# Fourier part: sequence first, and three of its seven products by seven smaller ones

## The chip, the core and the metric

The kernel runs on one core of a Trainium2 chip. The core has a matrix engine (TensorE, PE in the profile), three engines for element-wise work (VectorE or DVE, ScalarE or ACT, GpSimd or POOL), and a queue engine (SyncE or SP), which starts all of this kernel's transfers between HBM and the on-chip memory. The engines follow their own instruction lists and meet at semaphores. The metric is the device time of one execution in microseconds, the median of several runs.

## The reference, cut to what matters

Two independent computations are laid side by side in the output. All arrays are float32; S is 2048 and D is 1024.

```python
def _A_ref(x, wqkv, wo):                       # attention, 32 heads of 32
    qkv = (x @ wqkv).reshape(B, S, 3, H, Dh).transpose(2, 0, 3, 1, 4)
    q, k, v = qkv[0], qkv[1], qkv[2]
    p = _softmax(jnp.einsum("bhqd,bhkd->bhqk", q, k) * Dh ** -0.5)
    o = jnp.einsum("bhqk,bhkd->bhqd", p, v)
    return o.transpose(0, 2, 1, 3).reshape(B, S, D) @ wo

def _B_ref(x, dft_seq_re, dft_seq_im, dft_hid_re, dft_hid_im):   # Fourier mixing
    a = jnp.einsum("bsd,ed->bse", x, dft_hid_re)
    b = jnp.einsum("bsd,ed->bse", x, dft_hid_im)
    return jnp.einsum("ts,bse->bte", dft_seq_re, a) - jnp.einsum("ts,bse->bte", dft_seq_im, b)

return jnp.concatenate([_A_ref(...), _B_ref(...)], axis=-1)      # [1, 2048, 2048]
```

The Fourier part is the real part of (Cr + i Ci) X (Wr + i Wi), where X is 2048 x 1024, Cr and Ci are 2048 x 2048 and Wr and Wi are 1024 x 1024. It can be summed over the hidden dimension first, or over the sequence first.

## The kernel before

**Number form.** Each float32 operand of a large product is held as a high and a low half in a shortened float format (fp32r). One term of a product, a 128 x 128 block by a 128 x 512 block, is three matmuls: high by high, low by high, high by low. The halves are made by `halves`: a cast (line 528 on DVE, line 527 on ACT) and a subtraction (line 531 on POOL or DVE). `fetch` loads a block (line 491) and, where an operand is a sum of blocks, loads the others (line 500) and adds them (line 507 on POOL or DVE).

**Fast products.** Each large product is cut into 2 x 2 quarters and made with seven quarter products instead of eight, after Strassen and Winograd. This takes sums of operand quarters ahead of the products and sums of results behind them (`gather`).

**Stages.** Four pieces of matrix work are recorded in one long list, the fills: `qkv` (2016 matmuls), `dense1` (X by Wr and Wi, 448 terms, 1344 matmuls), `dense2` (Cr and Ci by the two results, 896 terms, 2688 matmuls) and `project` (the output projection of attention, 672 matmuls): 6720 in all. In the two Fourier stages a group of 12 or 24 matmuls sums one 128 x 512 result in a bank of PSUM, which DVE then drains. Operands, partial results and the result of `dense1` go through HBM buffers by transfers of 256 KB.

**Attention.** For every head two kinds of score matmuls are made (line 1322 for the row maxima, line 1447 for the exponentials), 4096 in all, and the products with V (line 1479), in 72 visits. DVE finds maxima, ACT takes exponentials, and both free the score banks.

**The order of the work.** A planner (`Plan`) is run when the program is recorded. It has a cost for each instruction, gives each engine's next instruction when its inputs will be there by these costs, and writes the engines' instruction lists. On PE it chooses at each step between the next fill and the next attention matmul; the fills are paced by `nf / (FILL - RES) <= done / ATT`, so that they last nearly as long as attention. On the chip the lists are fixed and every wait is a semaphore.

**The end.** `project` needs all heads. Its operand tiles use memory that attention held, so none of its loads may start before the last head's result is stored (`behind`, line 1519 stores it). Between the last visit to V and the first matmul of `project` PE has only what is left of `dense2`. `project` makes its seven products in the order 1, 7, 2, 6, 5, 3, 4, each with 8 groups of 12 matmuls. Product 1 uses eight tiles of the heads' outputs (`o_d`) and four of the weight (`wo`) as they are; for product 7 each of its eight and four tiles is a difference of two loaded blocks.

## Time and profile before

| | |
|---|---|
| median of 3 timed runs | 2941.32 us (2941.31 to 2941.8) |
| the profiled execution: span from its first to its last instruction | 2940.6 us |
| granted TensorE clock over the span | 1.000 |
| PE busy, share of the span | 2931.5 us, 100% |
| DVE, ACT, POOL busy | 77%, 77%, 33% |
| transfers | 587.96 MB, 61.8% of the 16 DMA engines' span |

The profiled execution's own time is known by its span; the lowest timed run is 0.7 us longer than that, which is what lies around the span. In the views, "PE" rows are matmuls and "PEld" rows the loading of their fixed operand. A matmul's listed duration (about 390 ns) is longer than its share of the engine, since matmuls overlap; the distance from one to the next is what counts. In a table by stretches, each engine has its busy time and, in brackets, its number of instructions; the last three columns are the granted clock, the busy share of the DMA engines and GB/s. Most groups carry the line of a helper: 421 is every product's matmul, whatever its stage.

### The profile page before, as it was taken

The page shows a single profiled execution, that of the slowest core. Times are in us where ns is not written, and L with a number is a line of the kernel's source. Part 1 is how long each engine was busy: PE and PEld are TensorE (multiplying, and loading weights), DVE is VectorE, ACT ScalarE, POOL GpSimd, SP SyncE. Part 2 cuts the span into 40 slices and gives each one's busy share as a digit, 9 for nine tenths or more (in the row PEclk, how much of TensorE's full clock was granted, in tenths as well). Part 3 has the DMA queues.
Part 4 walks back from the last instruction along what each step waited for, and adds up shares of the span by engine and source line. Part 5 has one row for each costly group of instructions (what it writes and reads, how often), then busy time and mean ns, then how long its engine had stood idle before and what let it go on. Part 6 is the DMA issues. An engine that isn't in the chain of part 4 may idle for free.

```text
span 2940.6 us, 45778 instructions
## 1 busy us (share of the span) xinstructions
PE 2931.5 (100%) x14922; PEld 2151.9 (73%) x14922; DVE 2275.1 (77%) x3103; ACT 2271.7 (77%) x4322; POOL 956.6 (33%) x746
## 2 busy tenths in 40 slices
...
GB/s 348 356 249 183 200 183 276 227 213 225 218 103 229 217 176 164 212 226 166 158 101 147 239 231 205 189 180 169 129 113 132 216 270 200 194 182 191 264 194 126
DMA packets 393880, 587.96 MB, mean 200 GB/s; under 512 B 112782, under 2 KB 114574, under 8 KB 393518
## 3 DMA queue, kind: packets, MB, share of 16 engines
q1 hardware_dynamic: 393644, 585.05, 61.8%
...
## 4 chain that ended last, share of the span: by engine, by line
PE 98%; DVE 1%; DMA 1%; ACT 0%; SPq 0%; issue 0%; DVEq 0%; ACTq 0%
PE pd L421 44%; PE psT L1447 16%; PE psS L1322 16%; PE pd L1479 15%; PE psT L421 6%; DVE negm L1328 0%; DMA er<-in_xa 0%; DVE l L531 0%; DMA qs<-qk_d 0%; PE psT L443 0%; ACT psS L1331 0%; DVE h L528 0%; PE pd L443 0%; ACT slot L527 0%; DVE slot L531 0%
## 5 line engine op out<-in xcount | busy, mean ns | idle before, releaser
L1328 DVE TENSOR_REDUCE negm<-psS 128x1 f32<-128x1024 f32 x1024 | 1242.8, 1221 | 226.4 <-PE psS L1322 215.2
L1331 ACT ACTIVATE psS<-psS,negm 128x1024 f32<-128x1024 f32 x1024 | 1223.9, 1195 | 71.8 <-DVE negm L1328 70.0
L421 PE MATMUL pd<-slot,h 128*128 128x512 f32 x3360 | 1144.0, 390 | 0.0
L1456 ACT ACTIVATE pt<-psT 128x512 f32<-128x512 f32 x1296 | 782.6, 697 | 260.1 <-PE psT L1447 237.2
L1447 PE MATMUL psT<-qs,ks 128*128 128x512 f32 x2048 | 794.3, 394 | 1.3 <-DMA qs<-qk_d 1.3
L421 PEld LDWEIGHTS pd<-slot,h 128*128 128x128 f32 x3360 | 630.7, 188 | 132.0
L421 PE MATMUL pd<-slot,l 128*128 128x512 f32 x1680 | 654.6, 390 | 0.0
L507 POOL TENSOR_TENSOR raw<-raw,g 128x512 f32<-128x512 f32 x295 | 382.6, 1304 | 483.8 <-DVE l L531 63.8
L1447 PEld LDWEIGHTS psT<-qs,ks 128*128 128x128 f32 x2048 | 381.8, 188 | 137.3 <-issue 45.3
L1322 PE MATMUL psS<-ks,qs 128*128 128x512 f32 x1552 | 473.4, 390 | 1.2 <-ACT psS L1331 1.2
L531 POOL TENSOR_TENSOR l<-raw,h 128x512 fp32r<-128x512 f32 x157 | 202.5, 1290 | 554.6 <-PE psT L1447 236.6
L531 POOL TENSOR_TENSOR slot<-raw,slot 128x512 fp32r<-128x512 f32 x156 | 201.0, 1293 | 518.0 <-DVE slot L528 146.3
L421 PEld LDWEIGHTS pd<-slot,l 128*128 128x128 f32 x1680 | 315.3, 188 | 67.0 <-issue 0.8
L1479 PE MATMUL pd<-pt,vt 128*32 128x512 f32 x2592 | 345.8, 594 | 0.0
L1322 PEld LDWEIGHTS psS<-ks,qs 128*128 128x128 f32 x1552 | 290.8, 188 | 64.0 <-ACT psS L1331 3.8
L1331 ACT ACTIVATION_READ_ACCUMULATOR psS<-psS,negm 128x1 f32 x1024 | 321.6, 314 | 0.0
L1456 ACT ACTIVATE ptm<-psT 128x512 f32<-128x512 f32 x392 | 242.6, 715 | 49.7 <-PE psT L1447 46.7
L1456 ACT ACTIVATE ptl<-psT 128x512 f32<-128x512 f32 x360 | 223.5, 708 | 31.0 <-PE psT L1447 30.2
L1479 PEld LDWEIGHTS pd<-pt,vt 128*32 128x32 f32 x2592 | 89.4, 110 | 180.3 <-issue 168.2
L421 PE MATMUL pd<-slot,slot 128*128 128x512 f32 x768 | 193.0, 391 | 0.0
L421 PEld LDWEIGHTS pd<-slot,slot 128*128 128x128 f32 x768 | 144.1, 188 | 31.2
L528 DVE CAST h<-raw 128x512 fp32r<-128x512 f32 x321 | 149.1, 467 | 14.5 <-PE pd L421 12.3
...
## 6 DMA issues: line engine op xcount, KB each, us to landing
...
g<-in_ct SPq DMA_DIRECT2D x128, 256.0 KB
...
qs<-qk_d SPq DMA_DIRECT2D x128, 192.0 KB
ks<-qk_d SPq DMA_DIRECT2D x128, 192.0 KB
...
```

What stands on the lines that cost most here:

```text
L421: nc.tensor.matmul(box["ps"], a[1]((a[0].hi, a[0].lo)[u]()), b[1]((b[0].hi, b[0].lo)[v]()), start=k == 0, stop=k == n - 1)
L507: return (nc.gpsimd if e == "POOL" else nc.vector).tensor_tensor(out=dest(), in0=dest() if a is None else a.get(), in1=other["q"] if "q" i ...
L528: return nc.vector.tensor_copy(hi(), raw())
L531: return (nc.gpsimd if e == "POOL" else nc.vector).tensor_tensor(out=lo(), in0=raw(), in1=f(hi()), op=ALU.subtract)
L1322: nc.tensor.matmul(p[:, i * NB : i * NB + NB], (QX[0] if own else QS[h % 2])[:, qt * P : qt * P + P], KS[h % 2][:, c * 1024 + i * NB : c * ...
L1328: nc.vector.tensor_reduce(out=ST["negm"][:, c, qt : qt + 1], in_=box["p"], axis=AX.X, op=ALU.max, negate=True)
L1331: nc.scalar.activation(box["p"], box["p"], AF.Exp, bias=ST["negm"][:, c, qt : qt + 1], accum_out=ST["sums"][:, c, qt : qt + 1])
L1447: nc.tensor.matmul(box["p"], KS[h % 2][:, t * P : t * P + P], QS[h % 2][:, j * NB : j * NB + NB], start=True, stop=True)
L1456: nc.scalar.activation(box["t"], box["p"], AF.Exp)
L1479: nc.tensor.matmul(po["p"][j * DH : j * DH + DH, :], VT[h][:, k, :], box["t"], start=(k == t0), stop=(k == t), tile_position=(0, j * DH),)
```

## The change

**What it does.** `dense1` now sums over the sequence: it makes U = X^T C^T for both Cr and Ci, a product of 1024 x 2048 by 2048 x 4096, whose result is stored in `ut_d` (the half of Ci with its sign turned). `dense2` then multiplies U^T by Wr and Wi, one product of 2048 x 2048 by 2048 x 1024, and its result goes to the output with no intermediate `y_d`. Together the two stages would again have 896 + 448 terms. Three of the seven products of `dense1` (`SPLIT = (1, 2, 3)`) are not made directly, in 4 x 4 groups of 8 terms (`simple`), but by seven products of their own quarters (`split`), in 7 x 2 x 2 groups of 4 terms: 112 terms in place of 128. The other four products keep their fixed operand, all eight tiles of it, on chip for the four column blocks (`held`). The running sums of the outer products go through HBM (`xx_d`, `yy_d`), the sums of the inner ones stay on chip. The pacing counts a fill of a split product 1.5 times (`HEAVY`), and casts may go to ACT there (`spare`).

```diff
-    ab_d = [[[dram.tile([P, NB], F32, name=f"ab_d{m}_{e}_{k}") for k in range(NS)] for e in range(2)] for m in range(2)]
-    y_d = [[dram.tile([P, NB], F32, name=f"y_d{i}_{e}") for e in range(2)] for i in range(NS)]
+
+    ut_d = [[[dram.tile([4, P, 4, P], F32, name=f"ut_d{e}_{n}_{r}") for r in range(2)] for n in range(4)] for e in range(2)]
...
-    FILL = 3 * (7 * 24 * 4 + 7 * 16 * 4 + 7 * 8 * 16 + 2 * 8 * 4)
+    SPLIT = (1, 2, 3)
+    HEAVY = 1.5
+    FILL = 3 * (7 * 24 * 4 + 7 * 16 * 8 - 16 * len(SPLIT) + 7 * 8 * 8 + 2 * 8 * 4)
...
-                fills.append((o, k == 0, n - k))
+                fills.append((o, k == 0, n - k, heavy[0]))
...
+    def merge(dst, acc, ps, kind, neg):
+
+        if not neg:
+            nc.vector.tensor_tensor(out=dst, in0=acc, in1=ps, op=kind)
+        elif kind == ALU.add:
+            nc.vector.scalar_tensor_tensor(out=dst, in0=ps, scalar=-1.0, in1=acc, op0=ALU.mult, op1=ALU.subtract)
+        else:
+            nc.vector.tensor_tensor(out=dst, in0=ps, in1=acc, op=ALU.subtract)
+
+    def put_out(to, t):
+
+        nc.sync.dma_start(to, t.rearrange("p (b j) -> p b j", b=4) if len(to.shape) == 3 else t)
...
+    def inner(j, x, y, outer, last_of):
...
+        def finish(ps, last):
+            def acc(A, B):
...
+            if j == 1:
+                return acc(x, None)
+            if j == 5:
+                return acc(y, x)
+            if j == 6:
+                acc(x, x)
+                return acc(y, y)
+            also = [acc(x, x)] if j == 7 else []
+            a = x if j in (2, 4) else y
+            box = {}
+            old, users = ER.take()
+
+            def emit():
+                box["y"] = pre.tile([P, NB], F32, name="e", tag="e", bufs=NE)
+                merge(box["y"], a.at(), ps(), ALU.subtract if j == 4 else ALU.add, outer[0] == 3)
+
+            e = done = evac_op(emit, last, ER, [users, a.users], [*old, a.last, *also])
+            if outer[0] != 1:
+                done = op("POOL", SUB, lambda e: (nc.gpsimd if e == "POOL" else nc.vector).tensor_tensor(
+                    out=box["y"], in0=box["y"], in1=got["c"], op=ALU.subtract if outer[0] == 3 else ALU.add),
+                    [e, c], [users, cusers], rank, other=("DVE", ADD, 20 + rank), two=True)
+            stored = op("SP", ISSUE, lambda: put_out(outer[2], box["y"]), [done], [users], rank, 256)
+            if outer[0] == 1:
...
+    def split_a(p, q, s1, s2):
+        return {
+            1: [(1, *q(0, 0))], 2: [(1, *q(0, 1))], 4: [(1, *q(1, 1))],
+            5: [(1, *q(1, 0)), (1, *q(1, 1))],
+            6: [(1, *s1), (-1, *q(0, 0))],
+            7: [(1, *q(0, 0)), (-1, *q(1, 0))],
+            3: [(1, *q(0, 1)), (-1, *s2)],
+        }[p]
+
+    def split_b(p, q, t1, t2):
...
+    OUTER = (1, 5, 2, 6, 7, 4, 3)
+    WITHIN = (1, 2, 5, 6, 7, 3, 4)
+    DONE_IN = {2: (0, 0), 7: (1, 1), 3: (0, 1), 4: (1, 0)}
...
+    def outer(p, X, Y, to, wrote, neg):
...
+        x = stored(X.first if p == 2 else X.kept) if p in (2, 4, 5, 6, 7) else None
+        y = stored(Y.kept) if p in (3, 6, 7) else None
...
+            if p == 1:
+                e = result(None, None, False, X.to[1], X)
+                X.first = X.kept
+                return e
+            if p == 5:
+                return result(x, ALU.add, False, Y.to[5], Y)
+            if p == 6:
+                result(x, ALU.add, False, X.to[6], X)
+                return result(y, ALU.add, False, Y.to[6], Y)
+            if p == 7:
+                result(y, ALU.add, neg, to, None)
+                return result(x, ALU.add, False, X.to[7], X)
+            return result(y if p == 3 else x, ALU.subtract if p == 4 else ALU.add, neg, to, None)
+
+        return finish
...
+    def dense1():
...
+        def to(h, m, n):
+            return ut_d[h[1]][n][h[0]][:, :, m, :].rearrange("b p j -> p b j"), ut_st[h[1]][n][h[0]]
...
+        def simple(p):
+            def a(m, k):
+                q = lambda r, kk: xq(4 * r + m, 8 * kk + 4 * k)
+                return split_a(p, q, (s1_d[m][k], s1[m][k]), (s2_d[m][k], s2[m][k]))
...
+            for n in range(4):
+                z = step[0]
+                step[0] += 1
+                M = []
+
+                def load(m, k):
+                    if n == 0:
+                        A[m, k] = held(fetch([P, 4, P], a(m, k), keep_a(m, k)), None if m < 2 else 12 + 2 * m + k)
+
+                for k in range(2):
+                    load(0, k)
+                    for c in range(4 * k, 4 * k + 4):
+                        M.append(moving((8 * z + c) % 12, b(n, c), keep_b(n, c)))
+                for m in range(1, 4):
+                    for k in range(2):
+                        load(m, k)
+                for m in range(4):
+                    h = DONE_IN.get(p)
+                    out_to = to(h, m, n) if h else (None, None)
+                    group(((chunk(A[m, k], c), (M[4 * k + c], whole)) for k in range(2) for c in range(4)), 8,
+                          outer(p, X[m][n], Y[m][n], *out_to, h is not None and h[1] == 1))
+                    if p == 7 and 3 in SPLIT and m % 2:
+                        i, k = divmod(2 * n + m // 2, 2)
+                        fetch([P, 4, P], [(1, *xq(i, 8 + 4 * k)), (-1, s2_d[i][k], s2[i][k])], (s4_d[i][k], s4[i][k]))
...
+        def split(i):
+            def base_a(m, k):
+                return (s4_d[m][k], s4[m][k]) if i == 3 else xq(m, 8 * (i - 1) + 4 * k)
+
+            def base_b(c, n):
+                return cq(*{1: (0, c), 2: (0, 8 + c), 3: (1, 8 + c)}[i], n)
...
+            x, y = accs(16) + accs(17), accs(18) + accs(19)
+            for j in WITHIN:
+                z = step[0]
+                step[0] += 1
+                A, M = [], {}
+                for n in range(2):
+                    A.append(piece(split_a(j, lambda r, k: base_a(2 * r + n, k), at(5, n), at(6, n)), at(j, n) if j in (5, 6) else None))
+                    for c in range(4):
+                        M[n, c] = moving((8 * z + 4 * n + c) % 12, split_b(j, lambda k, e: base_b(4 * k + c, 2 * e + n), at(5, n, c), at(6, n, c)),
+                                         at(j, n, c) if j in (5, 6) else None)
+                for n in range(2):
+                    for m in range(2):
+                        h = DONE_IN.get(j)
+                        outer = None
+                        if h:
+                            mm, nn = 2 * h[0] + m, 2 * h[1] + n
+                            outer = (i, X[mm][nn], xx_d[mm][nn][1], None) if i == 1 else (i, (Y if i == 3 else X)[mm][nn], *to(DONE_IN[i], mm, nn))
+                        group(((chunk(A[m], c), (M[n, c], whole)) for c in range(4)), 4, inner(j, x[2 * n + m], y[2 * n + m], outer, None))
+
+        for p in OUTER:
+            heavy[0] = HEAVY if p in SPLIT else 1.0
+            spare[0] = p in SPLIT
+            split(p) if p in SPLIT else simple(p)
+        heavy[0] = 1.0
+        spare[0] = False
...
+    def held(fetched, i):
...
     def dense2():
...
-                    to = out[t * P : t * P + P, D + e * NB : D + e * NB + NB] if m else y_d[t][e]
...
+        def load_ab(step, k):
+            p = ORDER[step]
+            AB[step, k] = moving((8 * step + k) % 12, moving_terms(p, lambda r, e: (wd[r, k, :, e * NB : e * NB + NB], []), (t2_d[k], t2[k])),
+                                 (t2_d[k], t2[k]) if p == 6 else None)
+
+        def a_terms(p, i, k0):
+            q = lambda r, k: (ut_d[k][2 * r + i // 4][k0 // 4][i % 4], ut_st[k][2 * r + i // 4][k0 // 4])
+            return base_terms(p, q, (s2_d[i][k0 // 4], s2[i][k0 // 4]))
...
+        for step, p in enumerate(ORDER):
...
+                h = DONE.get(p)
+                t, e = (8 * h[0] + i, h[1]) if h else (0, 0)
+                to = out[t * P : t * P + P, D + e * NB : D + e * NB + NB]
+                group(terms(), 8, gather(p, X[i // 2][i % 2], None, (u4_d[i], u4[i]), to, []))
...
-    done = 0.0
+    done = paid = 0.0
+    TO_PAY = sum(x[3] for x in fills[: FILL - RES])
...
-        if fill is not None and (not ok or (not first and left <= HB) or nf / (FILL - RES) <= done / ATT):
+        if fill is not None and (not ok or (not first and left <= HB) or paid / TO_PAY <= done / ATT):
             pl.start(fill)
             nf += 1
+            paid += weight
...
-        "xb": c(B_x[0].reshape(NS, P, NC, P).transpose(0, 3, 2, 1)),
+        "xb": c(B_x[0].reshape(NS, P, NC, P).transpose(2, 1, 0, 3)),
         "wd": c(np.stack([wr.T, wi.T]).reshape(2, NC, P, D)),
-        "ct": c(np.stack([cr, ci]).reshape(2, NS, P, NS, P).transpose(1, 4, 0, 3, 2).reshape(NS, P, 2 * NS, P)),
+        "ct": c(np.stack([cr.T, ci.T]).reshape(2, NS, P, S)),
```

**Where it moves instructions.** The planner writes every list anew from a little ahead of `dense1` on. Three places matter for the prediction.

First, PE around the last visit to V, the end of attention. Rows of 32x512 are the visit, rows of 128x512 on helper line 421 (417 after the change) are the fills; `ptm`, `ptl` and `pt` hold exponentials. Before:

```order
L1479 MATMUL pd<-pt,vt 32x512
L1479 MATMUL pd<-ptm,vt 32x512 x8
L1479 MATMUL pd<-ptl,vt 32x512 x5
L1479 MATMUL pd<-pt,vt 32x512 x18
L421 MATMUL pd<-slot_29598,l 128x512
L421 MATMUL pd<-slot_29598,h 128x512
```

With the change:

```order
L1691 MATMUL pd<-pt,vt 32x512
L1691 MATMUL pd<-ptm,vt 32x512 x8
L1691 MATMUL pd<-ptl,vt 32x512 x5
L1691 MATMUL pd<-pt,vt 32x512 x18
L417 MATMUL pd<-slot_30494,l 128x512
L417 MATMUL pd<-slot_30494,h 128x512
```

Behind the visit stand 161 matmuls of `dense2` before, and 53 with the change, ahead of the first matmul of `project`.

Second, SP's list at the loads for product 7 of `project`, with the change. `g<-o_d` is the second block of a head-output tile of product 7, `g<-in_wo` that of a weight tile, `a_..` is a block for a later product, and each transfer is 256 KB:

```order
L496 DMA g<-o_d_195 128x512
L487 DMA raw<-in_wo 128x512
L496 DMA g<-o_d_196 128x512
L496 DMA g<-in_wo 128x512
L487 DMA raw<-in_wo 128x512 x2
L487 DMA raw<-o_d_197 128x512
L487 DMA a_0_0_31453<-o_d_197 128x512
L487 DMA a_0_1_31460<-o_d_198 128x512
L496 DMA g<-in_wo 128x512 x3
```

Counted from the first load of `wo` behind the last head's store, the first `g<-in_wo` is transfer 37, the next three are transfers 43, 44 and 45. Before, they were transfers 55, 59, 62 and 63: the loads of `project` were the same ones, and 18 more transfers of `dense2` stood among them.

Third, POOL inside the second split product with the change, in its inner products 5 and 6. Line 503 (507 before) adds or subtracts two loaded blocks, line 527 (531 before) makes a low half:

```order
L503 TENSOR_TENSOR raw<-raw,g 128x512 x4
L527 TENSOR_TENSOR slot_14112<-raw,slot_14112 128x512
L503 TENSOR_TENSOR raw<-raw,g 128x512 x3
L527 TENSOR_TENSOR slot_14176<-raw,slot_14176 128x512
L503 TENSOR_TENSOR raw<-raw,g 128x512 x2
L527 TENSOR_TENSOR slot_14233<-raw,slot_14233 128x512
```

About as far into the program, in `dense1`, POOL's list before was this; line 1517 scales a head's result:

```order
L531 TENSOR_TENSOR l<-raw,h 128x512
L507 TENSOR_TENSOR raw<-raw,g 128x512
L1517 TENSOR_TENSOR ot<-ot,rt 128x512
L507 TENSOR_TENSOR raw<-raw,g 128x512 x2
L531 TENSOR_TENSOR slot_14123<-raw,slot_14123 128x512
```

The additions and low halves of the operands come in longer runs, with several instructions to a tile. Over the whole program the listing has 12732 instructions on PE in place of 12876, 934 instructions on POOL in place of 751, 3129 on DVE in place of 3105, 3365 on ACT in place of 3300 and 2840 on SP in place of 2546.

248 lines of the change are left out of this document (142 added, 106 removed).

## The prediction

> **What bounds the kernel now.** I read the engines' busy times first, then the chain of work that ended last, then a table by stretches of 75 us.
>
> ```profile
> PE 2931.5 (100%) x14922; PEld 2151.9 (73%) x14922; DVE 2275.1 (77%) x3103; ACT 2271.7 (77%) x4322; POOL 956.6 (33%) x746
> PE 98%; DVE 1%; DMA 1%; ACT 0%; SPq 0%; issue 0%; DVEq 0%; ACTq 0%
> q1 hardware_dynamic: 393644, 585.05, 61.8%
> ```
>
> PE is idle for 9.1 us of 2940.6, and 98% of the chain lies on it. Busy time alone proves little for PE, so the pace must be checked. The chain in order of time (start, duration, what) shows it:
>
> ```profile
> 27.35 5.44 PE psT L421 x24
> 2740.80 7.00 PE pd L1479 x64
> 2747.80 9.52 PE pd L421 x41
> 2779.08 8.16 PE psT L421 x36
> ```
>
> A group of 24 matmuls takes 5.44 us at the start, so one takes 0.2267 us, and the 36 at the end take 8.16 us, the same. PE has no slack inside a group and nearly none between groups. So this kernel's time is the number of matmuls by their pace, plus what PE waits, and each matmul removed is worth 0.2267 us unless another engine comes late.
>
> How close are the others to coming late? Columns: stretch, its length, then busy time and (instructions) of PE, PEld, DVE, ACT and POOL, the clock, the DMA share and GB/s.
>
> ```profile
> 75.00:150.00 75.00, 75.00 (x332) 62.12 (x331) 51.75 (x73) 26.17 (x45) 21.00 (x17) 1.00 1.00 358
> 1650.00:1725.00 75.00, 74.83 (x394) 53.26 (x393) 66.25 (x91) 63.60 (x124) 41.02 (x32) 1.00 0.86 277
> 2325.00:2400.00 75.00, 75.00 (x395) 53.15 (x394) 63.07 (x86) 64.05 (x123) 42.99 (x35) 1.00 0.83 263
> 2475.00:2550.00 75.00, 74.00 (x389) 51.93 (x388) 57.80 (x77) 62.16 (x119) 27.49 (x22) 1.00 0.54 168
> 2747.80:2788.00 40.20, 40.20 (x178) 33.27 (x179) 31.80 (x49) 9.37 (x15) 7.61 (x6) 1.00 0.91 323
> ```
>
> The second and third are the busiest stretches within attention, and PE lost 0.17 and 0.00 us in them. The worst of the four loads on DVE, ACT, POOL and DMA that this trace shows beside attention is therefore still hidden.
>
> **The removed work.** In the listing PE has 144 instructions fewer, all of them fills (6720 to 6576); scores, visits and the first 10 matmuls are the same in number. 144 x 0.2267 = 32.6 us. It is the only saving: both orders of summing have 1344 terms, and the split takes 16 terms of three matmuls from each of three products.
>
> *Beside the rows:* the Trainium skill, page "TensorE: Matmul & The Clock Gate", Part 1, gives 215.7 ns from one 512-column matmul to the next at full clock, so by it the sum would be 31.1 us. The trace has 226.7 ns, and the trace decides.
>
> **The added work on other engines.** The costs per instruction:
>
> ```profile
> L507 POOL TENSOR_TENSOR raw<-raw,g 128x512 f32<-128x512 f32 x295 | 382.6, 1304 | 483.8 <-DVE l L531 63.8 <-issue 48.2 <-DMA raw<-in_xb 44.9
> L531 POOL TENSOR_TENSOR slot<-raw,slot 128x512 fp32r<-128x512 f32 x156 | 201.0, 1293 | 518.0 <-DVE slot L528 146.3 <-DVE slot L531 78.0 <-PE pd L421 68.4
> L528 DVE CAST slot<-raw 128x512 fp32r<-128x512 f32 x228 | 103.1, 466 | 8.7 <-DMA raw<-ab_d 4.4 <-POOL raw L507 3.8
> L531 DVE TENSOR_TENSOR l<-raw,h 128x512 fp32r<-128x512 f32 x164 | 120.7, 740 | 3.1
> L527 ACT ACTIVATE slot<-raw 128x512 fp32r<-128x512 f32 x56 | 34.6, 631 | 79.5 <-DVE raw L507 20.1 <-DMA raw<-in_wo 17.3 <-PE psT L421 11.0
> ```
>
> POOL gets 183 more: 183 x 1.30 = 238 us, 957 to 1195 of some 2918. ACT gets 65 more casts, 65 x 0.63 = 41 us; DVE 24 more, under 18 us. SP starts 294 more transfers of 256 KB; one takes 262144 bytes / 358 GB/s = 0.73 us in the saturated stretch, or 0.81 us at the 323 GB/s of the last row of the stretches, so DMA goes from 61.8% of 2940.6 = 1817 us to some 2030 to 2060, 70%. All of this lies beside PE on the average, so it costs nothing where it is early.
>
> It is not even, though. I counted the listing in the three stretches in which the split products are prepared, 518 us together, placed by the matmuls ahead of them at the chain's pace. Per 75 us they hold 91 instructions on DVE, 40 on POOL and 88 transfers. DVE is as in the row 1650 to 1725 (91), and so are the transfers (the listing before has 88 for that row, whose share is 0.86). POOL is above anything in the trace: 40 x 1.30 = 52 us against 43. What stands behind a late POOL instruction is a tile's low half, and behind that a PE list that cannot turn to attention, because it is fixed.
>
> Bounds for these 518 us: nothing, by the row 2325 to 2400; and if each of the 21 inner products (3 x 7) starts one POOL subtraction late, 21 x 1.29 = 27 us. At the idle rates of 1650 to 1725 and of 2475 to 2550 (0.17 and 1.00 us per 75) it would be 1.2 to 6.9 us. I take the middle of these, **4 us**, since the loads are nearest to the first row. It cannot be below nothing here, because PE idles 9.1 us in the whole trace and most of that at its ends.
>
> **The end, where cover goes.** The change leaves 53 fills between the last visit and `project` in place of 161: 12.0 us in place of 36.5. These rows (time, duration, engine, what) give the chain that has to fit in it:
>
> ```profile
> 2747.92 0.69 DVE L1501 TENSOR_TENSOR ot<-ot,pd 128x512 f32<-128x512 f32 x1 [6.44 <-PE pd L1479]
> 2749.36 0.32 SPq L1519 DMA_DIRECT2D o_d<-ot  x1
> 2750.85 0.38 SPq L491 DMA_DIRECT2D raw<-in_wo  x1
> 2754.35 0.63 ACT L527 ACTIVATE slot<-raw 128x512 fp32r<-128x512 f32 x1 [11.88 <-DMA raw<-in_wo]
> 2786.44 0.68 DVE L507 TENSOR_TENSOR s<-s,g 128x512 f32<-128x512 f32 x1
> ```
>
> The visit ends at 2747.8. The first load of `wo` starts 3.1 us later, since it waits for the last head's store, and the tile's cast starts 3.5 us after its load. Product 1 needs its first weight and head tiles and then one more of each per 0.68 us; the fourth head tile is transfer 10: 3.1 + 9 x 0.77 + 3.5 + 0.63 = 14.2 us, and PE wants it at 12.0 + 3 x 0.68 = 14.0. So it just fits. Product 7 is different. PE wants its second term at 12.0 + 96 x 0.2267 + 0.68 = 34.4 us behind the visit. That term's weight tile is complete with transfer 43: 3.1 + 42 x 0.73 + 3.5 + 0.68 (difference) + 0.63 (cast) = 38.6 us, or 41.9 us at 0.81. PE waits 4.2 to 7.5 us. The lower bound is nothing, if the loads that stand between the first and the second `g<-in_wo` come sooner than I space them, as they may with fewer `dense2` transfers beside them. I take **5 us**. Before, transfer 59 stood against 36.5 + 22.4 = 58.9 us: 3.1 + 58 x 0.77 + 4.8 = 52.6, so it was covered. Behind product 7 each product has again 21.8 us for 20 or fewer loads (16 us), so nothing more is late.
>
> **The sum.** The profile's span is 2940.6 us, and the median lies 0.7 above it. 2940.6 - 32.6 + 4 + 5 = 2917.0 for a span, 2917.7 for a time: **2918 us**, 0.8% faster.
>
> **Rivals.**
>
> *All of the gain arrives.* POOL and the loads are early enough: 2941.3 - 32.6 = 2908.7. The row 2325 to 2400 speaks for it, the count of transfers at the end against it.
>
> *Each inner product starts late.* Groups of 12 matmuls in place of 24 need new tiles twice as often, and POOL's 40 per 75 us exceed what the trace has tried: 2908.7 + 27 + 0 to 5 = 2936 to 2941, which is no change. Against it speaks that DVE and ACT can take these instructions too, and that PE lost little at 35.
>
> *DVE and POOL block each other, and the kernel gets slower.* The trace shows that a two-input DVE instruction can wait for a POOL one:
>
> ```profile
> 2758.61 1.52 POOL L531 TENSOR_TENSOR slot<-raw,slot 128x512 fp32r<-128x512 f32 x1 [42.68 <-ACT slot L527]
> 2758.90 1.78 DVE L531 TENSOR_TENSOR l<-raw,h 128x512 fp32r<-128x512 f32 x1
> L531 DVE TENSOR_TENSOR e<-e 128x512 fp32r<-128x512 f32 x18 | 12.4, 687 | 0.6 <-POOL c L825 0.3
> ```
>
> It took 1.78 us in place of 0.69, 1.09 more. The split stretches hold 219 two-input instructions or casts on DVE. DVE is busy 66.25 of 75 us at the same number of instructions, so it has 0.117 x 518 = 60 us to spare there. For a slower kernel it would have to lose 60 + 32.6 + 5.9 = 98 us, 90 blocked instructions, 41% of the 219; at 60%, 131 x 1.09 - 60 = 83 us come back and the time is 2992. Now the mean of L531 on DVE is 0.740, 0.05 above the unblocked one, so 5% are blocked at a POOL load of 33%. At 69% of POOL 10% would be 24 us, within what is spare. The planner also orders the two by a semaphore where it expects them to meet.
>
> *Beside the rows:* the Trainium skill, page "SBUF — State Buffer", states that the pair of ports that DVE and GpSimd share is an exclusive lock for a whole instruction. The two rows above agree.
>
> *The clock falls in the new wait.* The matrix engine began at half its pace:
>
> ```profile
> L1555 PE MATMUL pd<-qs 96*128 96x512 f32 x10 | 4.6, 644 | 1.5 <-DVE qs L303 1.5
> ```
>
> Ten matmuls in 4.6 us are 0.46 each. If 5 us of waiting before product 7 bring that back for as long, 4.6 - 2.3 = 2.3 us are lost: 2920. *Beside the rows:* the Trainium skill, page "TensorE: Matmul & The Clock Gate", Part 1, states that the clock halves after an idle window of about 3.4 us. No stretch above shows a granted clock below 1.00.
>
> *The change does not remove what it says.* Excluded by the count.
>
> **Chances and range.** Forecast, with its waits of 2 to 18 us (2911 to 2927): 0.55. With the clock's fall added (2918 to 2930): 0.08. All of the gain (2907 to 2911): 0.13. Inner products late (2927 to 2941): 0.17. Blocking: 0.05; anything else, 0.02. The forecast's own range is 2910 to 2927. The range asked for leaves out the blocking and most of the late inner products' upper part: 2907 to 2933. About 0.2%, 5.9 us, is what a measurement tells from no change here: faster means under 2935.4, slower over 2947.2. Of the late inner products some two thirds lie under 2935.4, so faster is 0.55 + 0.08 + 0.13 + 0.11 + 0.01 = 0.88, no change 0.07, slower 0.05.
>
> **What would show it.** PE: 14778 matmuls and a pace of 24 in 5.44 us. POOL busy near 1195 us, DMA near 70%. In the chain, a piece that is not PE some 34 us behind the last visit, at the start of product 7, of 4 to 7 us: its absence shows that step wrong. In the table by stretches, PE some 0.2 to 1 us below the full length where the split products are prepared, about 770 to 950, 1160 to 1330 and 1930 to 2100 us; several us in one of them would be the late inner products, and L531's mean on DVE above 0.85 the blocking. A saving well below 20 us with no idle PE would make the whole reckoning by matmuls wrong.

## The result and the profile after

| | before | after |
|---|---|---|
| median | 2941.32 us (4 runs, 2940.9 to 2941.8) | 2957.45 us (4 runs, 2957.18 to 2959.18) |
| the profiled execution: span, and its time | 2940.6 us | 2955.7 us, 2957.53 us |
| granted clock over the span | 1.000 | 0.998 |

The ratio is 1.0058 (95% interval 1.0044 to 1.0073): the change makes the kernel 16 us **slower**; 2918 us had been predicted, and the range ended at 2933. The page of the changed kernel, busy times, transfers and the chain of waits by engine:

```profile
PE 2927.9 (99%) x14778; PEld 2119.8 (72%) x14778; DVE 2302.2 (78%) x3127; ACT 2308.7 (78%) x4387; POOL 1190.8 (40%) x929
q1 hardware_dynamic: 460556, 662.14, 69.6%
PE 90%; DMA 5%; ACT 3%; DVE 2%; issue 1%; SPq 0%; POOL 0%; DVEq 0%; POOLq 0%; ACTq 0%
```

PE has lost its 144 matmuls and is yet busy only 3.6 us less than before. Its idle time went from 9.1 to 27.8 us, and 8% of the chain have moved from PE to transfers, ACT and DVE. (1.8 us lie around the span in this execution, not 0.7: the 0.7 came from a timed run and the profiled one, which are two executions. So the medians differ by 16.1 us and the spans by 15.1.) What PE waits for, with the total in us, the number of waits and the longest:

```profile
PE psS L1534 <- ACT psS L1543: 9.6, 18, 1.2
PE psT L417 <- ACT slot L523: 4.9, 3, 3.5
PE psT L1659 <- ACT pt L1668: 3.6, 4, 1.8
PE pd L417 <- POOL slot L527: 2.1, 1, 2.1
```

Attention's rows (`psS` at 9.6 us, `pt` at 3.6) are mostly new, and the largest: PE waits more for ACT to free a bank of scores than for an operand of a fill. By stretches, first the kernel before and then the changed one (the three stretches in which it prepares and makes its split products, and the end):

```profile
750.00:1050.00 300.00, 300.00 (x1556) 216.94 (x1555) 231.76 (x313) 257.49 (x498) 90.10 (x71) 1.00 0.59 187
1200.00:1425.00 225.00, 225.00 (x1171) 163.85 (x1173) 172.28 (x229) 194.03 (x373) 51.38 (x40) 1.00 0.60 192
1950.00:2175.00 225.00, 225.00 (x1186) 161.63 (x1185) 176.84 (x243) 191.50 (x369) 62.42 (x49) 1.00 0.52 164
2725.00:2850.00 125.00, 125.00 (x585) 99.44 (x584) 93.81 (x138) 41.35 (x71) 32.71 (x25) 1.00 0.72 248
```

```profile
750.00:1050.00 300.00, 293.31 (x1498) 204.44 (x1497) 257.44 (x350) 254.76 (x488) 170.68 (x134) 0.99 0.85 279
1200.00:1425.00 225.00, 218.56 (x1117) 148.59 (x1110) 196.65 (x255) 193.95 (x372) 145.37 (x113) 1.00 0.93 299
1950.00:2175.00 225.00, 222.59 (x1160) 155.53 (x1160) 186.29 (x257) 198.61 (x385) 133.00 (x105) 1.00 0.76 232
2725.00:2850.00 125.00, 119.86 (x574) 88.48 (x573) 68.96 (x105) 53.09 (x94) 19.32 (x15) 0.97 0.54 183
```

PE loses 15.5 us in the three stretches and 5.1 us at the end. Busy time understates it: a matmul counts as busy for 390 ns and its successor should start after 227, so the first 0.16 us of each gap, and a half clock, look like work. So I measured from the start of each matmul to the start of the next in both traces. By this measure the kernel before, too, is 33 us over nominal, not 9.1. Time over 226.7 ns (218.8 in a V visit) I call **pace** where it is under 20 ns at a matmul, and **waits** otherwise:

| us over nominal | before | after | difference |
|---|---|---|---|
| 144 matmuls fewer | | | -32.6 |
| waits in the three stretches | 4.4 | 34.1 | +29.7 |
| waits behind 2725 us | 0.2 | 10.2 | +10.0 |
| waits elsewhere | 19.9 | 17.3 | -2.6 |
| pace | 8.4 | 19.0 | +10.6 |

The sum is +15.1 us, the difference of the spans. Three things have to be explained: the stretches, the end, and a pace that the prediction had taken as constant.

### The profile page after: what moved, and what is told of

It is laid out like the page before. It is cut to its first block, busy times and chain, and to the rows that moved or that the text cites. A ratio compares the mean times of both kernels' runs of the same rounds, so it can differ in the third digit from the quotient of the medians.

```text
span 2955.7 us, 46418 instructions
## 1 busy us (share of the span) xinstructions
PE 2927.9 (99%) x14778; PEld 2119.8 (72%) x14778; DVE 2302.2 (78%) x3127; ACT 2308.7 (78%) x4387; POOL 1190.8 (40%) x929
## 3 DMA queue, kind: packets, MB, share of 16 engines
q1 hardware_dynamic: 460556, 662.14, 69.6%
## 4 chain that ended last, share of the span: by engine, by line
PE 90%; DMA 5%; ACT 3%; DVE 2%; issue 1%; SPq 0%; POOL 0%; DVEq 0%; POOLq 0%; ACTq 0%
PE pd L417 41%; PE psT L1659 15%; PE psS L1534 15%; PE pd L1691 14%; PE psT L417 6%; ACT psS L1543 2%; DMA raw<-in_ct 1%; DVE negm L1540 1%; DMA t_d<-raw 1%; ACT pt L1668 1%; DMA ks<-qk_d 0%; DMA c<-xx_d 0%; DMA raw<-in_xb 0%; DMA g<-in_xb 0%; DMA yy_d<-e 0%
## 5 line engine op out<-in xcount | busy, mean ns | idle before, releaser
L417 PE MATMUL pd<-slot,h 128*128 128x512 f32 x2784 | 953.8, 391 | 2.4 <-POOL slot L527 2.1
L1668 ACT ACTIVATE pt<-psT 128x512 f32<-128x512 f32 x1296 | 776.1, 689 | 228.5 <-PE psT L1659 205.9
L1659 PE MATMUL psT<-qs,ks 128*128 128x512 f32 x2048 | 799.6, 396 | 3.6 <-ACT pt L1668 3.6
L503 POOL TENSOR_TENSOR raw<-raw,g 128x512 f32<-128x512 f32 x367 | 478.1, 1311 | 434.3 <-issue 69.3
L527 POOL TENSOR_TENSOR slot<-raw,slot 128x512 fp32r<-128x512 f32 x290 | 373.8, 1296 | 688.2 <-DVE slot L524 222.6
L417 PEld LDWEIGHTS pd<-slot,h 128*128 128x128 f32 x2784 | 523.2, 188 | 112.4 <-POOL slot L527 3.7
L417 PE MATMUL pd<-slot,l 128*128 128x512 f32 x1392 | 543.9, 391 | 0.2 <-DVE l L527 0.2
L1659 PEld LDWEIGHTS psT<-qs,ks 128*128 128x128 f32 x2048 | 382.2, 188 | 155.5 <-issue 45.3
L417 PE MATMUL pd<-slot,slot 128*128 128x512 f32 x1536 | 426.4, 394 | 0.0
L1534 PEld LDWEIGHTS psS<-ks,qs 128*128 128x128 f32 x1552 | 289.2, 188 | 77.0 <-ACT psS L1543 14.9
L417 PEld LDWEIGHTS pd<-slot,slot 128*128 128x128 f32 x1536 | 289.2, 188 | 65.5
L417 PEld LDWEIGHTS pd<-slot,l 128*128 128x128 f32 x1392 | 261.6, 188 | 56.2 <-issue 0.8
L1668 ACT ACTIVATE ptm<-psT 128x512 f32<-128x512 f32 x392 | 238.7, 698 | 44.7 <-PE psT L1659 40.6
L527 POOL TENSOR_TENSOR l<-raw,h 128x512 fp32r<-128x512 f32 x120 | 155.0, 1292 | 276.7 <-PE psT L1659 80.9
L1668 ACT ACTIVATE ptl<-psT 128x512 f32<-128x512 f32 x360 | 223.2, 706 | 34.9 <-PE psT L1659 34.2
L524 DVE CAST slot<-raw 128x512 fp32r<-128x512 f32 x375 | 186.8, 516 | 8.7 <-POOL raw L503 7.6
```

What stands on the lines that cost most here:

```text
L417: nc.tensor.matmul(box["ps"], a[1]((a[0].hi, a[0].lo)[u]()), b[1]((b[0].hi, b[0].lo)[v]()), start=k == 0, stop=k == n - 1)
L503: return (nc.gpsimd if e == "POOL" else nc.vector).tensor_tensor(out=dest(), in0=dest() if a is None else a.get(), in1=other["q"] if "q" i ...
L524: return nc.vector.tensor_copy(hi(), raw())
L527: return (nc.gpsimd if e == "POOL" else nc.vector).tensor_tensor(out=lo(), in0=raw(), in1=f(hi()), op=ALU.subtract)
L1534: nc.tensor.matmul(p[:, i * NB : i * NB + NB], (QX[0] if own else QS[h % 2])[:, qt * P : qt * P + P], KS[h % 2][:, c * 1024 + i * NB : c * ...
L1659: nc.tensor.matmul(box["p"], KS[h % 2][:, t * P : t * P + P], QS[h % 2][:, j * NB : j * NB + NB], start=True, stop=True)
```

## The experiments

All of them are timed beside the kernel before. The table has the median, its ratio with the 95% interval, and the same division of the profiled execution as above; the second group is built on the 13th run.

| run | median us | ratio | three stretches | end | elsewhere | pace |
|---|---|---|---|---|---|---|
| changed kernel | 2957.45 | 1.0058 [1.0044, 1.0073] | 34.1 | 10.2 | 17.3 | 19.0 |
| e1 no split | 2968.23 | 1.0096 [1.0080, 1.0111] | 7.8 | 8.2 | 19.0 | 23.6 |
| e2 later landing planned | 2998.59 | 1.0198 [1.0183, 1.0213] | 34.5 | 35.7 | 32.4 | 18.6 |
| e3 no casts on ACT | 2955.57 | 1.0049 [1.0033, 1.0066] | 39.8 | 3.7 | 17.7 | 18.0 |
| e4 product 7 halved | 2947.89 | 1.0024 [1.0014, 1.0034] | 29.1 | 2.9 | 18.2 | 19.2 |
| e5 32 bytes | 2954.31 | 1.0039 [1.0025, 1.0054] | 33.3 | 10.7 | 19.3 | 14.9 |
| e6 before, 32 bytes | 2941.21 | 1.0001 [0.9991, 1.0010] | 4.4 | 0.2 | 20.7 | 7.3 |
| e7 fewer loads | 2957.63 | 1.0053 [1.0038, 1.0068] | 20.3 | 19.7 | 17.7 | 18.7 |
| e8 fewer sums | 2980.77 | 1.0134 [1.0119, 1.0149] | 42.0 | 24.4 | 20.2 | 18.4 |
| e9 before, 144 fewer | 2929.74 | 0.9958 [0.9944, 0.9973] | 4.9 | 18.1 | 20.4 | 9.9 |
| e10 weight 1.0 | 2957.70 | 1.0055 [1.0040, 1.0070] | 31.3 | 9.1 | 18.2 | 20.0 |
| e11 weight 2.5 | 2957.01 | 1.0049 [1.0034, 1.0064] | 31.5 | 11.2 | 17.1 | 19.9 |
| e12 sides exchanged | 2980.77 | 1.0132 [1.0115, 1.0149] | 25.7 | 9.6 | 20.4 | 48.4 |
| e15 no round trip | 3003.19 | 1.0207 [1.0192, 1.0222] | 62.6 | 6.6 | 38.2 | 19.3 |
| e16 fewer loads, no trip | 2957.19 | 1.0054 [1.0037, 1.0071] | 25.9 | 17.1 | 18.5 | 18.9 |
| e13 slots on the right | 2948.34 | 1.0026 [1.0015, 1.0036] | 32.6 | 11.2 | 19.6 | 9.7 |
| e14 and no casts on ACT | 2949.28 | 1.0025 [1.0015, 1.0036] | 43.1 | 5.1 | 19.5 | 7.8 |
| e17 and five buffers | 2964.94 | 1.0085 [1.0070, 1.0100] | 41.8 | 4.1 | 29.8 | 10.4 |
| e18 and an early end | 2940.65 | 1.0001 [0.9991, 1.0010] | 32.7 | 3.1 | 16.8 | 9.3 |

e4, e7, e8, e9 and e16 leave out a part of the computation. Where the instructions ahead are the same (the changed kernel, e4, e5), the waits of the three stretches differ by up to 5 us from run to run, so only larger differences there are read.

### Which half of the change costs

```diff
-    SPLIT = (1, 2, 3)
+    SPLIT = ()
```

> Sequence first alone: the order of the Fourier part's two sums is the changed kernel's, but none of the seven products is made from quarters, so the 144 matmuls are back (14922). If the split's waits are the cause (its two inner-product stretches lost 14.0 and 14.2 us beside the kernel before), this run is at 2940 to 2944 us, as the kernel before, with waits of 0.3 us and over near 5 us in all. If the new order itself costs, by the slower pace (233 instead of 227 ns) of matmuls whose fixed operand stays in slots 16 to 19, seven such products lose about 10.6 x 7/4 = 19 us over nominal where before lost 8: about 2950 us. If both are wrong and the long preparation at the end is the whole loss, it is at 2950 us too, but with the loss behind 2780 us.

The new order of the sums alone is the worse half: 27 us slower than before, and the split takes 11 us of that off again. Its page has the same number of matmuls as before and 21 us more of busy PE:

```profile
PE 2952.7 (100%) x14922; PEld 2153.7 (73%) x14922; DVE 2229.8 (75%) x3023; ACT 2276.5 (77%) x4319; POOL 908.2 (31%) x709
```

15.2 us of its 25.7 are pace, 8.0 are at the end. So the split's own account is -32.6 + 26.3 (stretches) + 2.0 (end) - 4.6 (pace) - 1.7 = -10.6 us. The expectation of 2950 us had the pace, not the end with it.

### What a removed matmul is worth: the end

In the kernel before, one or two of a group's four blocks lose their third matmul, and the total by which the fills are paced is 144 lower:

```diff
-        n *= 3
+        n = 3 * n - less
...
-            for (u, v), after in (((0, 0), (a[0].made[0], b[0].made[0])), ((1, 0), (a[0].made[1],)), ((0, 1), (b[0].made[1],))):
+            for (u, v), after in (((0, 0), (a[0].made[0], b[0].made[0])), ((1, 0), (a[0].made[1],)), ((0, 1), (b[0].made[1],)))[: 2 if x < less else 3]:
...
+                        1 + (len(frees) % 7 < 2),
```

> The kernel before, with 144 matmuls of the Fourier part's first sum left out (the third of the three products of halves, in one or two of a group's four blocks; that part of the computation is left out) and nothing else changed. It measures the first term of the prediction by itself. In the order on PE the attention ends as late as before, and only 13 fill matmuls, 3 us, instead of 161, 36.5 us, stand between the last V visit and the output projection. If fewer matmuls are worth their PE time, 2941.3 - 32.6 = 2909 us. If the matmuls at the end were the cover of the projection's preparation, which takes some 40 us from the last V visit (by the run without quarters), 15 to 25 us of that come back as waits behind 2740 us: 2924 to 2934 us.

As forecast by the second theory: 12 us come out of 32.6. The long pieces of its chain (start, duration, what) behind the last V visit:

```profile
2744.26 7.00 PE pd L1480 x64
2751.26 3.18 PE pd L421 x13
2756.35 3.84 DMA raw<-in_wo
2761.59 3.49 DMA raw<-o_d
2767.33 5.05 DMA s<-o_d
2772.41 5.37 DMA t<-in_wo
2780.00 6.07 DMA raw<-in_wo
2786.09 4.21 DMA a<-o_d
2792.85 4.00 PE psT L421 x10
```

The last visit ends at 2751.3, 3.5 us later than before. The planner has put as many fills ahead of it as before (5891 against 5887), so all that was removed came out of the 161 fills that had covered the projection's loads. 17.9 us return as waits at the end. In the changed kernel 5851 fills stand ahead of the last visit: of the 144 removed, 108 came out of the cover. That visit ends at 2777.8 us, 30 us later than before, since PE has waited in the stretches and its pace is slower.

In the changed kernel, with a cover of 53 fills, the projection's seventh product is the one that comes late. This run makes its eight head-output tiles from one block:

```diff
-                7: lambda: [(1, *q(0, 0)), (-1, *q(1, 0))],
+                7: lambda: [(1, *q(0, 0))],
```

> The changed kernel, but the output projection's seventh product takes one block of head outputs instead of the difference of two: 8 transfers of 256 KB and 8 subtractions fewer (this part of the computation is left out). If the loss behind 2780 us (7.1 us of waits and 2.4 us of half clock) is the count of transfers against the 12 us of PE work that cover them, it falls to 1 to 4 us and the time to 2949 to 2953 us. If the wait ends on something else (the store and reload of the last head's output, or DVE's chain), the time stays within 1.5 us of 2957 us.

The end falls from 10.2 to 2.9 us, as the first theory has it. The time falls by 9.6, to 1 us below the expected range, since the stretches differ too, by the 5 us from run to run. So the loads of product 7, with the subtractions that went with them, are what came late. The number of fills alone does not tell how well the end is covered: e1 loses 8.2 us there behind 150 fills, and e15 6.6 behind 187. In e1 a head-output block was loaded only 34.3 us behind the last visit (`2802.51 5.34 DMA raw<-o_d` in its chain, the visit ending at 2768.2), and PE stood in product 1 until it had been cast.

### The pace

Each operand's address was taken from the built program and put beside the trace. The fills' operands lie on the right side of the on-chip memory (160 to 224 KB of each partition), as do attention's query and key tiles. Slots 16 to 19 lie on the left, at 38 to 54 KB, and `held` puts half of the fixed tiles of a `simple` product there. In e1, between 900 and 1900 us, a fill whose own and whose successor's fixed operand lie there starts its successor after 233.8 ns on average (564 cases); where both lie on the right it is 227.2 ns (560 cases). Attention's score matmuls beside the former are at 230 ns.

```diff
     rec = const.tile([P, 2 * NS], F32, name="rec")
+    const.tile([P, 8], F32, name="pad")
```

> The changed kernel with one unused tile of 32 bytes per partition ahead of everything on the left side of the memory. In the runs so far a matmul that reads an operand from the left side (slots 12 to 19, whose addresses divide by 64) starts its successor after 233 to 236 ns, and one whose operands are both on the right (addresses with a remainder of 32) after 227 ns: 1152 such matmuls in the changed kernel, 1728 in the run without quarters, 384 in the kernel before. If the remainder does it (operands that lie differently against 64 bytes), the pad takes it away: 227 ns everywhere, and 10 to 11 us less, 2945 to 2948 us. If it is the side or the distance, or what else happens while these tiles are in use, nothing changes: 2956 to 2959 us.

> The same 32 bytes in the kernel before, as a control: 384 of its matmuls read an operand from the left side, all between 450 and 720 us, where 4.4 us of pace are lost. If the remainder against 64 bytes does it, 3 to 5 us less, 2936 to 2938 us; if not, 2941 us.

Between the two: 4.1 us of pace go, with 3.1 us of time, and 230.4 ns stay where 233.8 were. In the kernel before 1.1 us of pace go and the time does not change. The next run keeps the 32 bytes.

```diff
-    big = ctx.enter_context(tc.tile_pool(name="big", bufs=1, side="right"))
+    big = ctx.enter_context(tc.tile_pool(name="big", bufs=1))
-    parts = ctx.enter_context(tc.tile_pool(name="parts", bufs=1, side="right", reuse_waits="tile"))
-    pre = ctx.enter_context(tc.tile_pool(name="pre", bufs=1, reuse_waits="tile"))
+    parts = ctx.enter_context(tc.tile_pool(name="parts", bufs=1, reuse_waits="tile"))
+    pre = ctx.enter_context(tc.tile_pool(name="pre", bufs=1, side="right", reuse_waits="tile"))
```

> The changed kernel with the 32 bytes of the pad, and with two groups of buffers exchanged: the operand slots 0 to 11 and the ring of fixed operands go to the left side of the memory, the buffers in which transfers land and sums are made go to the right. If operands on the left are slow because the transfers and sums work there, the pace is 227 to 228 ns everywhere: 2954 - 7 = 2947 us. If a change between sides from one matmul to the next is what costs (attention's operands stay on the right, all fills are now on the left), the pace gets worse everywhere: 2970 us and more. If only the address against 64 bytes counts, it stays near the pad's 2954 us.

Slower by 23 us, with 29 us more of pace. The output projection shows it without attention beside it: nearly every matmul has now one operand on the left and one on the right. The chain of this run, and behind it that of the changed kernel:

```profile
2843.86 5.60 PE pd L418 x24
2939.06 5.60 PE psT L418 x24
```

```profile
2834.89 5.44 PE pd L417 x24
2938.25 5.44 PE psT L417 x24
```

5.60 / 24 = 233.3 ns against 226.7, from the addresses alone. That transfers and sums work on the left is not it, since those buffers had been moved away. In the same run, 44 fills with both operands on the left are at 226.7 ns. The run that follows from this puts slots 16 to 19 on the right, at 128 to 144 KB:

```diff
-            return late["sums" if i > 15 else "low"].tile(shape, dt, name=f"slot{i}", tag=f"slot{i}")
+            return late["held" if i > 15 else "low"].tile(shape, dt, name=f"slot{i}", tag=f"slot{i}")
...
+            late["held"] = ctx.enter_context(tc.tile_pool(name="held", bufs=1, side="right", reuse_waits="tile"))
```

> The changed kernel, with slots 16 to 19 on the right side of the memory, where all other operands of the fill matmuls and the scores are; to make room, the tiles of the exponentials lie lower, and four operand slots of the output projection use the query and key tiles of the attention, which has ended by then. The order of the work is the same. If operands on two sides are what slows the pace, the 10.6 us go: 226.7 to 227.5 ns in the Fourier part and 2946 to 2949 us. If something else about the products that use these slots does it, 2955 us and more.

```profile
PE 2918.6 (99%) x14778; PEld 2118.6 (72%) x14778; DVE 2308.8 (78%) x3127; ACT 2306.5 (78%) x4387; POOL 1188.7 (40%) x929
```

With the order of the work as it was, the pace falls from 19.0 to 9.7 us, PE is busy 9.3 us less, and the time falls by 9.1 us. That is 9 of the 10.6 us. From 900 to 2100 us, a fill on these slots that another such fill follows starts it after 227.3 ns, where the changed kernel has 233.9 (437 cases each, waits left out).

### The waits of the three stretches

The planner counts a transfer as landed 1.6 us after its turn in the queue. By my reading of the trace, a large transfer takes mostly 4.2 to 5.3 us from its issue in the split stretches (medians of 75 us windows), and mostly 3 to 3.9 in the same stretches before. On the chain one such place stands out: a sum for an inner product goes out and comes back before PE can go on.

```profile
838.10 5.91 DMA w_d<-raw
844.07 5.09 DMA raw<-w_d
849.18 0.70 DVE raw L503
849.91 0.63 ACT h L523
850.54 0.49 ACT pt L1668
```

The last two lines show how the lateness reached PE. The next exponential stood behind the late cast in ACT's list, and PE waited 1.8 us for that exponential (`PE psT L1659 <- ACT pt L1668`), not for the tile. It is so in most places. In the three stretches of the changed kernel the trace puts 12.5 us of PE's waits down to ACT and 2.3 us to a fill's tile. Two rows of the stretch from 1200 to 1425 us, of PE and of ACT:

```profile
PE psS L1534 <- ACT psS L1543: 5.1, 10, 0.8
ACT slot L523 <- DMA raw<-in_ct: 4.2, 2, 3.9
```

ACT and DVE together wait 32.8 us in the three stretches for loaded blocks, sums and halves of operands; in the kernel before it is 3.8 us, and without the split (e1) nothing. Attention's instructions stand behind these waits.

Four runs leave the work as it is and change the plan:

```diff
-    LANDING = 1.6
+    LANDING = 3.6
```

> The changed kernel, with one number of the planner changed: it takes a transfer to land 3.6 us after its slot in the queue instead of 1.6 us. If late transfers cause the waits (issue to landing 5.0 to 5.3 us in the split stretches, by my reading of the trace), preparations are ordered earlier or their users later, the gaps of 0.3 us and over fall from 29.5 to 10 to 15 us, and the time to 2940 to 2948 us. If the transfers cannot be earlier because the DMA engines are full (97 and 98% in two windows) or because there is no free buffer, it stays within 3 us of 2957 us, or is slower.

```diff
-            spare[0] = p in SPLIT
+            spare[0] = False
```

> The changed kernel, but in the three split products no cast may go to ACT: all go to DVE. If ACT, which runs casts between the attention's exponentials, holds up PE in those stretches, the time falls by 4 to 8 us, to 2950 to 2953 us. If late transfers are the cause, the time stays within 2 us of 2957 us. If DVE is the bound there (91 of 75 us's work in operations per 75 us in the prediction's stretches, now some 12 more casts of 0.52 us), it is slower by 5 to 15 us.

```diff
-    HEAVY = 1.5
+    HEAVY = 1.0
```

> The changed kernel, with the planner's weight of a matmul of the split products at 1.0 instead of 1.5: these products run closer together, and their transfers with them. If late transfers cause the waits, there are more: the excess of the three stretches goes from 33.6 us to 40 us or more, and the time to 2962 us or more. If the density of transfers has no part in it, 2955 to 2960 us.

And with `HEAVY = 2.5` in the same place:

> The changed kernel, with that weight at 2.5: the split products are spread over a longer piece of the attention, with fewer transfers per microsecond. If late transfers cause the waits, the excess of the split stretches falls from 33.6 us to 15 to 25 us, and the time to 2940 to 2950 us. If not, 2955 to 2960 us.

None of them helps in the stretches: 34.5, 39.8, 31.3 and 31.5 against 34.1 us. A later landing in the plan leaves no fills at all for the end, and 36 us are lost there. ACT's casts alone are not the cause: without them the stretches lose 5.7 us more, and e3 is 2 us faster only because 89 fills are left for the end, which loses 6.5 us less. DVE has 69 instructions more in e3, so that run does not rule DVE out.

Four runs change the work in the stretches. In the first two, `cut[0]` is true in the split products, inside `fetch`:

```diff
+            if cut[0]:
+                sign, q, gusers = 1, None, []
+                other["k"] = Kept(dest)
```

> The changed kernel, where in the three split products a sum or difference of two blocks takes the first block twice: its POOL addition stays and the load of the second block is left out (so this part of the computation is too): 120 transfers of 256 KB fewer, a quarter of those in these stretches. If transfers that land late cause the waits there (33.6 us over nominal in the three stretches, against 6 in the kernel before at the same times), that falls to under 15 us, and the time by 15 us or more, to under 2943 us if the end stays as it is. If POOL's additions or the port that it shares are the cause, it stays above 27 us there, and the time within 5 us of 2957 us.

```diff
+                if cut[0]:
+                    gusers.append(q)
+                    continue
```

> The counterpart: in the three split products the second blocks are loaded as before and not added (this part of the computation is left out): some 120 POOL additions of 1.3 us fewer, no transfer fewer. If late transfers are the cause, the excess of the three stretches stays above 25 us and the time within 6 us of 2957 us; if POOL or its port is, the excess falls to under 15 us and the time to under 2943 us. If each does half, both runs fall by about 10 us.

With 120 loads fewer, 14 us of the waits go, and 20.3 are left, between the two expectations. With 95 POOL instructions fewer none do; they rise, and the time, 2981 us, lies far above what I had expected. The time of e7 stays, because its order leaves only 15 fills for the end, where 9.5 us more are lost. So loads have a part in it, and POOL's load by itself is not shown to have one. The waits of ACT and DVE for operands move the same way: 20.8 us in e7 and 40.6 in e8. In e8 DVE's casts stand right behind the loads, as in this row of its first stretch, and ACT waits 39.9 us for DVE's maxima (20.0 in the changed kernel):

```profile
DVE slot L528 <- DMA raw<-in_ct: 12.8, 6, 5.9
```

In e2, e3 and e14 the two do not go together: 18.0, 13.2 and 13.4 us of such waits, and 34.5, 39.8 and 43.1 us on PE. So this path is in the traces, but it is not shown to be the whole. The sum rows of the three stretches, of the changed kernel, of e7 and of e8:

```profile
sum 750.00, PE 734.47 PEld 508.57 DVE 640.38 ACT 647.32 POOL 449.05; mean PE 244.82 PEld 169.52 DVE 213.46 ACT 215.77 POOL 149.68
```

```profile
sum 750.00, PE 741.33 PEld 524.58 DVE 635.70 ACT 651.58 POOL 393.14; mean PE 247.11 PEld 174.86 DVE 211.90 ACT 217.19 POOL 131.05
```

```profile
sum 750.00, PE 723.84 PEld 510.77 DVE 602.57 ACT 619.74 POOL 337.76; mean PE 241.28 PEld 170.26 DVE 200.86 ACT 206.58 POOL 112.59
```

```diff
-                    A.append(piece(split_a(j, lambda r, k: base_a(2 * r + n, k), at(5, n), at(6, n)), at(j, n) if j in (5, 6) else None))
+                    A.append(piece(fresh_a(j, lambda r, k: base_a(2 * r + n, k))))
...
+                        M[n, c] = moving((8 * z + 4 * n + c) % 12, fresh_b(j, lambda k, e: base_b(4 * k + c, 2 * e + n)))
```

`fresh_a` and `fresh_b` write the sums of inner products 6, 3 and 4 out in input blocks.

> The changed kernel, where the third, fourth and sixth inner product make their sums from the input blocks again instead of loading sums that the fifth and sixth have stored: per split product some 30 loads and 30 additions more and 20 stores fewer. If the round trip (a store of 5.9 us and a load of 5.1 us stood on the chain of waits at 840 us) is what makes PE wait, the waits of the three stretches fall from 34 to 20 us or less and the time to 2945 us or less. If the number of transfers does it, they rise, and the time is 2957 to 2970 us.

The other run is e7 with input blocks in place of the stored sums:

> The run with fewer loads (a block added to itself instead of a second block, which leaves that part of the computation out), now also without storing and reloading the inner sums. That run had 20 us of waits in the three stretches, against 34 in the changed kernel and 4 in the kernel before. If the rest is the round trip, it falls to under 10 us. If it is something that comes with the added additions and evacuations themselves, it stays at 15 to 25 us.

The round trip is refuted as the rest: e16 has 25.9 us of waits against 20.3 in e7. In e15, with more loads and additions to a tile, the waits rise to 62.6 us and the time to 3003 us, well above the 2970 expected, while the DMA engines are less busy than in the changed kernel (0.80, 0.80 and 0.64 against 0.85, 0.93 and 0.76):

```profile
750.00:1050.00 300.00, 289.63 (x1454) 196.56 (x1453) 257.19 (x344) 262.56 (x504) 182.46 (x144) 0.99 0.80 256
1200.00:1425.00 225.00, 213.69 (x1080) 139.96 (x1072) 189.54 (x243) 195.43 (x375) 144.82 (x114) 0.99 0.80 251
1950.00:2175.00 225.00, 219.02 (x1128) 149.10 (x1126) 179.73 (x239) 195.20 (x375) 118.22 (x94) 1.00 0.64 197
```

So a full queue alone does not explain it. e7 and e15 have in common that the waits go with the loads and steps that a tile's preparation takes. Its landing buffer is held through its loads, its additions and its two halves, and there are six such buffers; I took the time that a buffer is held for what limits. e8, where a buffer is held through fewer additions, does not fit that. On top of e13, one of them is taken away:

```diff
-NRAW, NHL, NG = 6, 4, 4
+NRAW, NHL, NG = 5, 4, 4
```

> The run with slots 16 to 19 on the right (2948.3 us), with five landing buffers instead of six. In the order on PE 139 instead of 53 fill matmuls now stand between the last V visit and the output projection, since the planner gives the attention more of the time where buffers are short. If the time that a buffer is held limits the preparations, the waits of the three stretches grow from 33 to 40 us or more; the end's 11 us fall to 2 us by its longer cover (31.5 us); together 2945 to 2955 us. If buffers do not limit, the waits stay at 33 us and the time falls by the end's 9 us, to 2937 to 2941 us.

With one buffer fewer the waits of the stretches grow from 32.6 to 41.8 us with the same work, though in another order, and those elsewhere from 19.6 to 29.8; the time, 2965 us, is above what I had expected, since I had not counted the latter. The end, with 139 fills, loses 4.1 instead of 11.2 us. So buffers matter, but an order changed for another reason can move the stretches as much (e14, below), and no run has more than six: that the time a buffer is held is the limit at six is argued and not shown.

> The same, with no casts on ACT in the split products. That alone took 2 us off and left 89 instead of 53 matmuls between the last V visit and the output projection: 2944 to 2947 us if the two add up.

That run is e13 without the casts on ACT. The two gains do not add up: the stretches lose 10 us more and the end 6 us less. DVE again has 69 instructions more.

### A version that takes two of the causes away

On top of e13, the projection loads into the common landing buffers and not into its own, which lie where attention's tiles were, so that its loads need not wait for attention's end:

```diff
-            last = op("SP", ISSUE, lambda: nc.sync.dma_start(dest(), first[0]), old + first[1] + gate, [users], rank, 256, raws if keep is None else None)
+            last = op("SP", ISSUE, lambda: nc.sync.dma_start(dest(), first[0]), old + first[1] + (gate if keep is not None else []), [users], rank, 256, raws if keep is None else None)
...
-                q = op("SP", ISSUE, load, gold + term[1] + gate, [gusers], rank, 256, seconds)
+                q = op("SP", ISSUE, load, gold + term[1], [gusers], rank, 256, seconds)
...
-        where[0] = (Ring(5), Ring(4), lambda shape, name, n: op_pool().tile(shape, F32, name=name, tag=name, bufs=n), over)
+        where[0] = (*where[0][:3], over)
```

> The run with slots 16 to 19 on the right (2948.3 us), where the output projection loads into the common six landing buffers instead of five buffers of its own, which lie where the attention's tiles were: its first loads need not wait for the attention's end. The order on PE is the same, with 53 fill matmuls of cover. If the late start of these loads is the end's loss, its 11 us fall to 3 to 7 us: 2940 to 2944 us. If the sums, casts and slots that follow, which still wait for the attention's tiles, set the end, it stays at 2947 to 2950 us.

```profile
2775.31 5.48 DMA raw<-o_d
2782.22 1.44 PE psT L422 x5
2783.66 5.46 PE pd L422 x24
```

The end loses 3.1 instead of 11.2 us, and the median is 2940.65 us: 16.8 us below the changed kernel and level with the kernel before. The stretches' 33 us are still in it. No run of the whole computation is faster than the kernel before.

## Why the prediction was wrong

**What held.** 14778 matmuls; POOL at 1190.8 us (1195 predicted); DMA at 69.6% (70%). Matmul groups away from attention are still at 5.44 us.

Three terms of the sum were mis-sized: the stretches by 25.7 us, the pace by 10.6 and the end by 5.0, less 2.6 elsewhere. That is the 38.7 us between the predicted and the measured span.

**"Each matmul removed is worth 0.2267 us"** took the pace of the matmuls that remain for fixed. `held` puts 768 more matmuls on slots 16 to 19 (384 before, 1152 after), which slowed them and their neighbours: +10.6 us, a term that the sum put at nothing; e13, which moves these slots, takes 9.3 of it away. The rows at 5.44 us that I read the pace from had all their operands on one side. That matmuls removed from a cover are worth less was in the prediction, as its term for the end; e9 shows how far it can go, 12.0 us gained of 32.6.

**"I take the middle of these, 4 us"** was 29.7 us, above even the upper bound of 27. This is the step that failed worst. The 4 us came from PE's idle time in stretches with as many DVE instructions and transfers per 75 us. That is a count of work, and it left out that the lists are in order: where a block lands late or its sum is late, the casts of ACT and DVE wait for it, attention's maxima and exponentials wait behind them, and PE waits for those (12.5 us of its listed waits, against 2.3 for a tile). The trace shows this path; e2, e3 and e14 show that it is not all. Why the blocks are late is shown in part: fewer loads take 14 us away, more loads and steps per tile add 28.5. That six buffers are the limit is not shown. The rival of late inner products was nearest in size (27 us), and the sign for it, "several us in one of them", is in the rows above. Its mechanism, a late POOL subtraction in each inner product, is not what the trace has: PE waits for a low half of POOL's once there, for 2.1 us.

**"I take 5 us" for the end** was 10.0. The place was right: product 7, some 35 us behind the last visit. So was the wait itself: by the starts it is 5.0 us. What the sum lacked is the half clock behind it, some 3 us, and 1.3 us in product 1. These rows give it:

```profile
2770.75 7.00 PE pd L1691 x64
2777.75 6.80 PE pd L417 x29
2784.55 5.46 PE psT L417 x24
2817.35 0.69 DVE t L503
2818.07 0.64 ACT slot L523
2818.75 4.50 PE psT L417 x9
2823.25 6.20 PE pd L417 x24
```

PE's longest wait there, 3.5 us in the second row of its waits, is product 7's first tile, where the prediction had the second one late; shorter ones follow, and the clock falls. Loads issued between 2780 and 2815 us took 5.3 us to land (median), where the prediction had a cast 3.5 us behind its load. The 24 matmuls in 6.20 us include the end of that, 0.76 over the usual 5.44. So the rival of the falling clock came on top of the wait and was no alternative to it. Product 1, which "just fits", lost the 1.3 us.

**The blocking of DVE and POOL** did not come, by its own sign, a mean of the low halves on DVE above 0.85 us. The changed kernel's row has 0.740, as before:

```profile
L527 DVE TENSOR_TENSOR slot<-raw,slot 128x512 fp32r<-128x512 f32 x194 | 139.8, 740 | 13.8 <-ACT slot L523 13.0
```

**The clock.** Stretches of the changed kernel right behind two of PE's waits, with the granted clock third from the end:

```profile
851.80:855.20 3.40, 3.40 (x9) 2.65 (x9) 2.14 (x2) 2.70 (x6) 3.23 (x3) 0.50 0.92 343
2817.90:2824.70 6.80, 6.04 (x14) 4.30 (x14) 5.16 (x10) 1.83 (x3) 1.28 (x1) 0.50 0.99 340
```

The trace has it at 0.50 for 3.41 us from 851.8 and for 6.83 us from 2817.9. A wait of 2.0 us, by the starts, went ahead of the first; another of 2.2 us at 974 us brought no fall. The Trainium skill, page "TensorE: Matmul & The Clock Gate", Part 1, has the clock fall after an idle window of about 3.4 us, and the windows run freely. The length of the falls agrees with that; a wait that is shorter than a window sufficed once and once did not.

**What stays open.** With fewer loads, 20 of the 34 us of waits are still there (4 before). Fewer DVE operations were not tried, and DVE is busy 85% of these stretches (77% before); where it got more (e3, e14), PE waited longer. So DVE's load is a rival that stands. Whether late blocks cost anything if attention's instructions did not stand behind their casts was not tested either. Nor was why the planner leaves as many fills ahead of attention's end when fills are taken away; ACT is busy for 86% of the three stretches, in both kernels.
